# Letting GpSimd's weight differences wait for VectorE's sums of x, and moving one VectorE addition ahead of an h product

## The chip, the cores and the metric

The kernel runs on one core of one Trainium2 chip. The metric is device microseconds of one execution, the median over runs. A core has five engines with their own instruction queues: TensorE (PE, matmuls; PEld are its weight loads), VectorE (DVE), ScalarE (ACT), GpSimd (POOL) and SyncE (SP, which only issues DMAs here). Engines wait for each other through semaphores.

## What is computed

The reference is a retention recurrence (4 batches, 8 heads, 768 positions, head size 64) whose output, as 3072 tokens of width 512, goes through a bilinear feed-forward layer with hidden width 1536. The change lies wholly in the second half:

```python
def _attn_ref(q, k, v):
    ...
    for t in range(S):
        state = gamma * state + einsum('bhd,bhe->bhde', k[:, :, t], v[:, :, t])
        y[:, :, t] = scale * einsum('bhd,bhde->bhe', q[:, :, t], state)
    return y

def _moe_ref(x, w_a, w_b, w_out):
    a = x @ w_a
    b = x @ w_b
    return a * b @ w_out
```

## The kernel before

Tokens are taken in chunks of 128; 24 chunks form eight blocks J = 0..7 of 4, 2, 2, 2, 2, 4, 4, 4 chunks. For each block the recurrence (in a chunked form) leaves x transposed in the tile `xt[J]`. Then come 12 slices ft of the hidden width: `ffn_a` computes a = x·w_a into a PSUM bank and ScalarE copies it to `asb`; `ffn_g` computes g = x·w_b and VectorE multiplies the two into `ht` (line 629, called the h product below). The output stage `ffn_fast` multiplies `ht` with w_out for a pair of chunks at a time, u = 0, 1, by a scheme with seven products for eight; it needs four kinds of sums of `ht`, the tiles `hsum` (`add`, line 684, kinds 0 to 3), and adds the products up with VectorE and ScalarE through `snap` and `osb`.

Blocks 6 and 7 use the seven-product scheme for a = x·w_a too, for slices 2f and 2f+1 with f = 1..5. Its operands are

- the sums of x, `xs`: four VectorE additions and subtractions of `xt` (`combine_x`, line 695), for block 6 in the middle of the last output stage of block 5 (visit `(5, "sums", 1)`), for block 7 at its start;
- the differences of w_a, `ta`: four GpSimd subtractions for each f (`combine_a`, line 704), 20 in all, made once, from the visit `(5, "late", 0)` on.

`seven_a(J, f)` issues seven pairs of matmuls (`part_a`) into three banks R1, R2, R5, with two products g between them. `behind` holds what of one f is put behind the first matmuls of the next f: a VectorE addition (`plus(odd[:, W2:], R1, snap[:, 2])`, line 742) that reads the bank R1, and `last_of`, which adds part 4 into the same R1 and copies it out. Behind the last f there is no next one, so `seven_end` issues what is left, with the last two g between. `sums_of` gives the `hsum` of f − 1 to GpSimd; for block 6 all of them (f = 0 and 1 in one go of width 512), for block 7 those of f = 0 to 3 and kinds 0 and 1 of f = 4, VectorE doing the rest.

The order on each engine is the order of the code: `seq` ties every instruction to the one before it on its engine. The table `ahead` lists what is put in at named places (`visit`). `gate` makes the next GpSimd instruction wait for the VectorE instruction that was issued last; it stood in front of the vb casts of `(5, "late", 0)` before.

A PSUM bank is written anew only when its last reader is done. So in the output stage of block 5, u = 1, TensorE's last product, `product(R1, J, u, ("h", 1, 1), ...)`, waits for `plus(osb[:, 1, DH:], R1, snap[:, 3])`, which in VectorE's queue stands behind the four sums of x; and in `seven_end`, part 4 waits for the addition out of `behind`.

Of the kernel before, what the change touches and what calls it, by code (L numbers as in the profile page):

```python
# [12 lines left out]
ALU = mybir.AluOpType  # L13
# [14 lines left out]
def kernel(  # L28
# [10 lines left out]
    nc = tc.nc  # L39
# [38 lines left out]
    def seq(bi):  # L78
        ins = bi.ins
        if gates and ins.engine == mybir.EngineType.Pool:  # L80
            tc.add_manual_dep(ins, gates.pop(), after, reason="behind VectorE's sums")
        prev = last.get(ins.engine)
        if prev is not None:
            tc.add_manual_dep(ins, prev.name, nosync, reason="program order")
        last[ins.engine] = ins
        return bi
# [101 lines left out]
    def late_tables():  # L188
        seq(nc.gpsimd.memset(mask, 1.0))
        for c in range(2):  # L190
            mc = mask[64 * c : 64 * c + 64]
            seq(nc.gpsimd.affine_select(out=mc, in_=mc, compare_op=ALU.is_ge, fill=0.0, base=0,
                                        pattern=[[0, 1], [1, 2], [2, D // 2]],
                                        channel_multiplier=-1))
        return positions([[P, NCH], [0, 1]], 1), positions([[P, NCH], [0, 1]], 2, True)

    late = late_tables()
# [81 lines left out]
    def catch_up(n=100):  # L279
        for fn in later[:n]:  # L280
            fn()
        del later[:n]
# [5 lines left out]
    sums = {}  # L288
# [283 lines left out]
    def xcols(J, kt, c0, c1):  # L572
        W2 = 2 * P
        x = xt[J][:, c0 // W2 : (c1 + W2 - 1) // W2, kt].rearrange("p u par m -> p u (par m)")
        return x if c1 - c0 > W2 else x[:, 0, c0 % W2 : c0 % W2 + c1 - c0]
# [14 lines left out]
    ht = {}  # L590

    asbs = {}

    def parts(J, ft, c0, c1):

        if J == 0 and 2 <= ft < 10:
            return [(c0, (c0 + c1) // 2), ((c0 + c1) // 2, c1)]
        return [(c0, c1)]

    def ff_bank(J, ft, c, name):  # L600

        if (J, ft) in SPARE:
            return psat.tile([P, 4 * P], F32, tag=f"y{c}", name=name)
        return psff.tile([P, 4 * P], F32, tag="ff", name=name)

    def ffn_a(J, ft, c0=0, c1=None):
        c1 = TILES[J] * P if c1 is None else c1
        if J not in ht:
            ht[J] = htp.tile([P, NFT, 4 * P], BF16, tag="ht", name="ht")
        fs = slice(ft * P, (ft + 1) * P)  # L610
        a = ff_bank(J, ft, 0, "a")[:, : c1 - c0]
        for kt in range(KT):
            for b0, b1 in parts(J, ft, c0, c1):
                seq(nc.tensor.matmul(a[:, b0 - c0 : b1 - c0], wa_bf[:, kt, fs], xcols(J, kt, b0, b1),  # L614
                                     start=(kt == 0 and b0 == c0), stop=(kt == KT - 1 and b1 == c1),
                                     skip_group_check=True))
        asb = asbs[J, ft, c0] = asbp.tile([P, 4 * P], BF16, tag="asb", name="asb")[:, : c1 - c0]
        seq(nc.scalar.copy(asb, a))  # L618

    def ffn_g(J, ft, c0=0, c1=None):  # L620
        c1 = TILES[J] * P if c1 is None else c1
        fs = slice(ft * P, (ft + 1) * P)
        g = ff_bank(J, ft, 1, "g")[:, : c1 - c0]
        for kt in range(KT):
            for b0, b1 in parts(J, ft, c0, c1):
                seq(nc.tensor.matmul(g[:, b0 - c0 : b1 - c0], wb_bf[:, kt, fs], xcols(J, kt, b0, b1),  # L626
                                     start=(kt == 0 and b0 == c0), stop=(kt == KT - 1 and b1 == c1),
                                     skip_group_check=True))
        seq(nc.vector.tensor_tensor(ht[J][:, ft, c0:c1], g, asbs.pop((J, ft, c0)), op=ALU.mult))  # L629

    def ffn_ab(J, ft):
        ffn_a(J, ft)
# [6 lines left out]
    def store():  # L639
        for dst, src in held:  # L640
            seq(nc.sync.dma_start(out=dst, in_=src))
        held.clear()
# [45 lines left out]
    def combine_x(J):  # L688
        xs[J] = raw.tile([P, 4, 2, 2 * P], BF16, tag="q" * (J == 6) + "k" * (J == 7) + "f", name="xs")
        a11, a12, a21, a22 = (xt[J][:, u, 2 * c : 2 * c + 2].rearrange("p k par m -> p k (par m)")  # L690
                              for u in range(2) for c in range(2))
        s1, s2, s3, s4 = (xs[J][:, i] for i in range(4))
        for dst, x, y, op in ((s1, a21, a22, ALU.add), (s2, s1, a11, ALU.subtract),
                              (s4, a12, s2, ALU.subtract), (s3, a11, a21, ALU.subtract)):
            seq(nc.vector.tensor_tensor(dst, x, y, op=op))
# [12 lines left out]
    def own_banks(J):  # L708
        at = psat.tile([P, 2, 4 * P], F32, tag="at", name="a")
        st = psst.tile([P, 4 * P], F32, tag="st", name="a")  # L710
        y = [psat.tile([P, 4 * P], F32, tag=f"y{c}", name="a") for c in range(2)]
        banks[J] = [[y[f % 2][:, : 2 * P], st[:, : 2 * P], at[:, f % 2, : 2 * P]] for f in range(2)]

    def part_a(J, f, R, which, first):
        u, c, r, i = {1: (0, 0, 0, None), 2: (0, 1, 0, None), 3: (None, 1, 1, 3), 4: (1, 1, 3, None),
                      5: (None, None, 0, 0), 6: (None, None, 1, 1), 7: (None, None, 2, 2)}[which]
        for k in range(2):
            if which > 3:
                w = ta[r][:, k, f]
            else:  # L720
                w = wa_bf[:, 2 * c + k, (2 * f + r) * P : (2 * f + r + 1) * P]
            if i is None:
                x = xt[J][:, u, 2 * c + k].rearrange("p par m -> p (par m)")
            else:
                x = xs[J][:, i, k]
            seq(nc.tensor.matmul(R, w, x, start=(first and k == 0), stop=(k == 1),  # L726
                                 skip_group_check=True))

    def seven_a(J, f):

        W2 = 2 * P
        if J not in banks:
            own_banks(J)
        R1, R2, R5 = banks[J][f % 2]
        if (J, f) == (6, 1):
            R5 = psff.tile([P, 4 * P], F32, tag="ff", name="a")[:, :W2]
        snap = raw.tile([P, 4, W2], F32, tag="vf", name="snap")
        even, odd = (asbp.tile([P, 4 * P], BF16, tag="asb", name="asb") for _ in range(2))
        asbs[J, 2 * f, 0], asbs[J, 2 * f + 1, 0] = even, odd

        def plus(dst, R, x):
            seq(nc.vector.tensor_tensor(dst, R, x, op=ALU.add))  # L742

        part_a(J, f, R1, 1, True)
        seq(nc.scalar.copy(snap[:, 0], R1))  # L745
        part_a(J, f, R2, 2, True)
        part_a(J, f, R5, 5, True)
        seq(nc.scalar.copy(snap[:, 2], R5))
        for fn in behind[:1]:
            fn()  # L750
        plus(even[:, :W2], R2, snap[:, 0])
        catch_up(2)
        ffn_g(J, 2 * f - 1)
        part_a(J, f, R1, 6, False)
        seq(nc.scalar.copy(snap[:, 1], R1))
        for fn in behind[1:]:
            fn()
        behind.clear()
        part_a(J, f, R5, 3, False)
        plus(odd[:, :W2], R5, snap[:, 1])  # L760
        catch_up(2)
        ffn_g(J, 2 * f - 2)
        part_a(J, f, R1, 7, False)

        def last_of():
            part_a(J, f, R1, 4, False)
            seq(nc.scalar.copy(even[:, W2:], R1))

        behind.extend((lambda: plus(odd[:, W2:], R1, snap[:, 2]), last_of))

    behind = []

    def seven_end(J, f):
        behind[0]()
        ffn_g(J, 2 * f + 1)
        behind[1]()
        behind.clear()
        ffn_g(J, 2 * f)

    def product(R, J, u, left, right, first):  # L780
# [181 lines left out]
    for j in range(NO):  # L962
# [14 lines left out]
        (5, 0): [(casts, 20, "kq")], (5, 2): [(casts, 21, "kq"), (casts, 20, "v"), (casts, 21, "v")],  # L977
        (5, 3): [(turn, 16, None)], (5, 5): [(casts, 22, "kq")],
        (5, 6): [(casts, 23, "kq")], (5, 8): [(turn, 18, 16)],
        (5, "late", 0): [(gate,), (casts, 22, "v"), (casts, 23, "v")] + [(combine_a, f) for f in range(1, 6)],  # L980
        (5, "sums", 0): [(turn, 20, 18)], (5, "sums", 1): [(combine_x, 6)],
        (6, "a", 0): [(turn, 22, 20), (deal, 1, 0, 2, 3, 4), (catch_up, 2), (mask_now,)],
        (6, "o", 0): [(turn, None, 22)],
    }
# [18 lines left out]
    def blocks_seven(J):  # L1003
        f0, f1 = SEVEN[J]
        if J == 7:
            combine_x(J)
        store()
        for ft in range(2 * f0):
            ffn_a(J, ft)
            visit(J, "a", ft)  # L1010
        for f in range(f0, f1):
            seven_a(J, f)
            sums_of(J, f - 1)
            mask_now(1)
        seven_end(J, f1 - 1)
        sums_of(J, f1 - 1)
        return 2 * f1
# [77 lines left out]
```

## Time and profile before

| | |
|---|---|
| runs shown | 219.76, 219.34, 219.76 us; median 219.76 us |
| the profiled execution's own time | 219.66 us |
| its span, first to last instruction | 218.0 us, so 1.66 us lie around it |
| granted TensorE clock | 1.00 of full speed over the whole span |

Time by stage, busy microseconds of each engine:

| stretch, us | what runs | length | PE | DVE | ACT | POOL |
|---|---|---|---|---|---|---|
| 144.0 to 153.6 | output of block 5, sums of x, differences of w_a | 9.60 | 8.28 | 8.26 | 4.27 | 8.75 |
| 153.6 to 175.1 | block 6: a and g, recurrence of chunks 20 to 23 | 21.50 | 21.33 | 15.52 | 10.34 | 16.68 |
| 175.1 to 184.9 | output of block 6 | 9.80 | 9.80 | 4.49 | 3.53 | 3.81 |
| 184.9 to 205.0 | block 7: a and g | 20.10 | 20.00 | 15.24 | 7.99 | 11.69 |
| 205.0 to 218.0 | output of block 7, and the end | 13.00 | 9.47 | 4.58 | 2.98 | 0.00 |

A row of the timeline gives the start and the length of an instruction (or of several merged, with their count), engine, line, what is written and read, and in brackets the idle time ahead of it and what ended it. A row of the chain of waits gives start, length, engine, tile and line of one piece of the work that ended last. A matmul's length reaches past the start of the next one, since matmuls are pipelined.

### The profile page before, as it was taken

The page shows a single profiled execution, that of the slowest core. Times are in us where ns is not written, and L with a number is a line of the kernel's source. Part 1 is how long each engine was busy: PE and PEld are TensorE (multiplying, and loading weights), DVE is VectorE, ACT ScalarE, POOL GpSimd, SP SyncE. Part 2 cuts the span into 40 slices and gives each one's busy share as a digit, 9 for nine tenths or more (in the row PEclk, how much of TensorE's full clock was granted, in tenths as well). Part 3 has the DMA queues.
Part 4 walks back from the last instruction along what each step waited for, and adds up shares of the span by engine and source line. Part 5 has one row for each costly group of instructions (what it writes and reads, how often), then busy time and mean ns, then how long its engine had stood idle before and what let it go on. Part 6 is the DMA issues. An engine that isn't in the chain of part 4 may idle for free.

```text
span 218.0 us, 7107 instructions
## 1 busy us (share of the span) xinstructions
PE 209.2 (96%) x2886; PEld 157.0 (72%) x2889; DVE 147.5 (68%) x326; ACT 97.7 (45%) x247; POOL 129.5 (59%) x199
## 2 busy tenths in 40 slices
PE   6789999999999999999999999998999999999993
PEld 6578896785478888888887445486666588666682
DVE  2783547648938877786794587979577753777731
ACT  3675244342436446446475253735555242444231
POOL 6557789682737447572827573759929980087400
PEclk9999999999999999999999999999999999999999
DMA  5999999998998998899979899932200002200022
GB/s 171 347 376 383 370 310 381 357 206 174 238 234 195 292 256 179 200 266 189 188 164 273 187 276 215 203 75 98 101 0 0 3 0 99 98 2 3 0 96 96
DMA packets 94832, 39.77 MB, mean 182 GB/s; under 512 B 76112, under 2 KB 91728, under 8 KB 94800
## 3 DMA queue, kind: packets, MB, share of 16 engines
q1 hardware_dynamic: 94656, 39.20, 69.3%
q8 instruction: 22, 0.36, 0.7%
q10 hardware_dynamic: 144, 0.13, 0.2%
q14 instruction: 10, 0.08, 0.1%
HBM read 28.31 MB, written 6.29 MB: 159 GB/s over the span
## 4 chain that ended last, share of the span: by engine, by line
PE 90%; DMA 3%; DVE 2%; POOL 1%; ACT 1%; issue 1%; SPq 0%; POOLq 0%; DVEq 0%
PE g L626 28%; PE o L788 22%; PE a L614 21%; PE a L726 7%; PE o L661 5%; DMA kf<-in_k_dram 3%; PE y L375 2%; POOL kqb L245 1%; PE y L387 1%; PE at L330 1%; PE st L300 1%; DVE ht L629 1%; PE y L545 1%; PE tp L466 1%; PE st L507 1%
## 5 line engine op out<-in xcount | busy, mean ns | idle before, releaser
L629 DVE TENSOR_TENSOR ht<-g,asb 128x256 bf16<-128x256 f32 (+1 forms) x98 | 53.6, 548 | 36.4 <-PE g L626 29.9
L626 PE MATMUL g<-xt,wb_bf 128*128 128x256 bf16 (+1 forms) x424 | 77.7, 311 | 0.0
L614 PE MATMUL a<-xt,wa_bf 128*128 128x256 bf16 (+1 forms) x344 | 56.9, 295 | 0.1
L618 ACT CAST asb<-a 128x256 bf16<-128x256 f32 (+1 forms) x78 | 34.5, 443 | 47.6 <-PE a L614 46.3
L626 PEld LDWEIGHTS <-wb_bf 128*128 128x128 bf16 x424 | 41.3, 98 | 15.7
L614 PEld LDWEIGHTS <-wa_bf 128*128 128x128 bf16 x344 | 33.0, 98 | 10.9 <-DVE xt L209 0.4
L248 POOL TENSOR_TENSOR kqb<-kf,ktab 128x256 bf16<-128x256 f32 x28 | 17.5, 644 | 26.0 <-DMA kf<-in_k_dram 18.2
L788 PEld LDWEIGHTS <-hsum 128*128 128x128 bf16 x240 | 23.2, 98 | 2.9
L684 POOL TENSOR_TENSOR hsum<-ht 128x256 bf16<-128x256 bf16 (+1 forms) x19 | 13.7, 719 | 18.2 <-DVE ht L629 18.2
L800 ACT COPY snap<-o 128x256 f32<-128x256 f32 x38 | 14.2, 374 | 21.6 <-PE o L788 21.2
L209 POOL CAST vb<-vf 128x512 bf16<-128x512 f32 x30 | 17.9, 628 | 10.0 <-DMA vf<-in_v_dram 7.2
L788 PE MATMUL o<-wt_bf,hsum 128*128 128x256 bf16 x180 | 21.9, 273 | 0.0
L788 PEld LDWEIGHTS <-ht 128*128 128x128 bf16 x180 | 17.2, 98 | 4.6 <-issue 1.5
L248 POOL TENSOR_TENSOR kqb<-qf,qtab 128x256 bf16<-128x256 f32 x28 | 17.2, 635 | 3.6 <-DMA qf<-in_q_dram 3.5
L314 DVE TENSOR_TENSOR sums<-st,sums 128x256 f32<-128x256 f32 x30 | 12.7, 424 | 5.0 <-PE st L300 3.7
L788 PE MATMUL o<-wo_bf,ht 128*128 128x256 bf16 x120 | 14.9, 273 | 0.0
L207 ACT CAST gst<-sums 128x256 bf16<-128x256 f32 x33 | 12.8, 412 | 0.5 <-DVE sums L312 0.3
L803 DVE TENSOR_TENSOR osb<-o,snap 128x256 f32<-128x256 f32 x22 | 9.1, 416 | 5.6 <-ACT snap L800 3.7
L742 DVE TENSOR_TENSOR asb<-a,snap 128x256 bf16<-128x256 f32 x30 | 11.9, 418 | 1.1 <-ACT snap L745 0.9
L245 POOL TENSOR_TENSOR kqb<-kf,ktab 128x512 bf16<-128x512 f32 x7 | 7.7, 1107 | 8.0 <-DMA kf<-in_k_dram 7.7
L726 PEld LDWEIGHTS <-ta 128*128 128x128 bf16 x80 | 7.8, 98 | 6.1 <-issue 0.8
L336 DVE TENSOR_TENSOR aT<-at,mask 128x512 bf16<-128x512 f32 x18 | 12.1, 679 | 0.0
(100 smaller groups left out, 288.3 us busy)
## 6 DMA issues: line engine op xcount, KB each, us to landing
out_dram<-osb SPq DMA_DIRECT2D x11, 512.0 KB, 4.8
kf<-in_k_dram SPq DMA_DIRECT2D x18, 256.0 KB, 4.0
qf<-in_q_dram SPq DMA_DIRECT2D x36, 128.0 KB, 3.6
vf<-in_v_dram SPq DMA_DIRECT2D x18, 256.0 KB, 4.2
wsta<-in_moe_w_a_dram SPq DMA_DIRECT2D x6, 512.0 KB, 7.6
wstb<-in_moe_w_b_dram SPq DMA_DIRECT2D x6, 512.0 KB, 7.9
wsto<-in_moe_w_out_dram SPq DMA_DIRECT2D x6, 512.0 KB, 9.3
kf<-in_k_dram SPq DMA_DIRECT2D x3, 512.0 KB, 5.9
```

Source lines behind the costliest of these rows:

```text
L207: seq(nc.scalar.copy(dst, src))
L209: seq(engine.tensor_copy(dst, src))
L248: seq(eng.tensor_tensor(dst[:, r], src[:, r], tab[:, r], op=ALU.mult))
L314: seq(nc.vector.tensor_tensor(new, u[c][:, s], old, op=ALU.add))
L614: seq(nc.tensor.matmul(a[:, b0 - c0 : b1 - c0], wa_bf[:, kt, fs], xcols(J, kt, b0, b1), start=(kt == 0 and b0 == c0), stop=(kt == KT - 1 a ...
L618: seq(nc.scalar.copy(asb, a))
L626: seq(nc.tensor.matmul(g[:, b0 - c0 : b1 - c0], wb_bf[:, kt, fs], xcols(J, kt, b0, b1), start=(kt == 0 and b0 == c0), stop=(kt == KT - 1 a ...
L629: seq(nc.vector.tensor_tensor(ht[J][:, ft, c0:c1], g, asbs.pop((J, ft, c0)), op=ALU.mult))
L684: seq(eng.tensor_tensor(s[which], x(), y(), op=op))
L726: seq(nc.tensor.matmul(R, w, x, start=(first and k == 0), stop=(k == 1), skip_group_check=True))
L788: seq(nc.tensor.matmul(R[:, :DH], lhs, (wo_bf, wt_bf)[w][:, f, m, :], start=(first and f == 0), stop=(f == NH - 1), skip_group_check=True))
L800: seq(nc.scalar.copy(snap[:, i], R[:, :DH]))
```

## The change

Two edits.

1. In `ahead`, the sixteen GpSimd subtractions for f = 2 to 5 move from `(5, "late", 0)` to `(5, "sums", 1)`, behind `combine_x(6)` and a new `gate`. So GpSimd makes those of f = 1, and then waits for the fourth sum of x.
2. In the last `seven_a` of blocks 6 and 7 (`ends`), the addition from R1 is no longer left to `seven_end`: it is issued ahead of the h product of slice 2f − 2 = 8, which stood ahead of it.

```diff
-    def ffn_g(J, ft, c0=0, c1=None):
+    def ffn_g(J, ft, c0=0, c1=None, now=True):
...
-        seq(nc.vector.tensor_tensor(ht[J][:, ft, c0:c1], g, asbs.pop((J, ft, c0)), op=ALU.mult))
+        asb = asbs.pop((J, ft, c0))
+
+        def times():
+            seq(nc.vector.tensor_tensor(ht[J][:, ft, c0:c1], g, asb, op=ALU.mult))
+
+        if not now:
+            return times
+        times()
...
-    def seven_a(J, f):
+    def seven_a(J, f, ends=False):
...
-        ffn_g(J, 2 * f - 2)
+        times = ffn_g(J, 2 * f - 2, now=not ends)
         part_a(J, f, R1, 7, False)
...
         behind.extend((lambda: plus(odd[:, W2:], R1, snap[:, 2]), last_of))
+        if ends:
+            behind.pop(0)()
+            times()
...
     def seven_end(J, f):
-        behind[0]()
         ffn_g(J, 2 * f + 1)
-        behind[1]()
-        behind.clear()
+        behind.pop()()
         ffn_g(J, 2 * f)
...
-        (5, "late", 0): [(gate,), (casts, 22, "v"), (casts, 23, "v")] + [(combine_a, f) for f in range(1, 6)],
-        (5, "sums", 0): [(turn, 20, 18)], (5, "sums", 1): [(combine_x, 6)],
+        (5, "late", 0): [(gate,), (casts, 22, "v"), (casts, 23, "v"), (combine_a, 1)],
+        (5, "sums", 0): [(turn, 20, 18)], (5, "sums", 1): [(combine_x, 6), (gate,)] + [(combine_a, f) for f in range(2, 6)],
...
-            seven_a(J, f)
+            seven_a(J, f, f == f1 - 1)
```

GpSimd's queue around the differences of w_a, before: the four `ta` tiles (3374 to 3377) of f = 1, then those of f = 2; in brackets what a row waits for.

```order
L209 CAST vb_3106<-vf_2962 128x512 [waits DMAHW0_49,PE_49]
L704 TENSOR_TENSOR ta_3374<-wa_bf_172 128x2x128
L704 TENSOR_TENSOR ta_3375<-wa_bf_172,ta_3374 128x2x128 [waits Pool_49]
L704 TENSOR_TENSOR ta_3376<-wa_bf_172 128x2x128
L704 TENSOR_TENSOR ta_3377<-wa_bf_172,ta_3375 128x2x128 [waits Pool_49]
L704 TENSOR_TENSOR ta_3374<-wa_bf_172 128x2x128
L704 TENSOR_TENSOR ta_3375<-wa_bf_172,ta_3374 128x2x128 [waits Pool_49]
```

And of the change:

```order
L209 CAST vb_3106<-vf_2962 128x512 [waits DMAHW0_49,PE_49]
L711 TENSOR_TENSOR ta_3374<-wa_bf_172 128x2x128
L711 TENSOR_TENSOR ta_3375<-wa_bf_172,ta_3374 128x2x128 [waits Pool_49]
L711 TENSOR_TENSOR ta_3376<-wa_bf_172 128x2x128
L711 TENSOR_TENSOR ta_3377<-wa_bf_172,ta_3375 128x2x128 [waits Pool_49]
L711 TENSOR_TENSOR ta_3374<-wa_bf_172 128x2x128 [waits DVE_49]
L711 TENSOR_TENSOR ta_3375<-wa_bf_172,ta_3374 128x2x128 [waits Pool_49]
```

The queue holds the same instructions in the same order; the first one of f = 2 has gained a wait for VectorE, which is the fourth sum of x.

VectorE's queue at the end of block 7's stretch (`asb` 4390 is the odd half of f = 5, g 4416, 4427 and 4436 are those of slices 8, 11 and 10), before:

```order
L742 TENSOR_TENSOR asb_4390<-a_4224,snap_4388 128x256 [waits PE_49,Activation_49]
L629 TENSOR_TENSOR ht_4209<-g_4416,asb_4349 128x512 [waits PE_49,Activation_49]
L742 TENSOR_TENSOR asb_4390<-a_4227,snap_4388 128x256 [waits PE_49]
L629 TENSOR_TENSOR ht_4209<-g_4427,asb_4390 128x512 [waits DVE_49,PE_49]
L629 TENSOR_TENSOR ht_4209<-g_4436,asb_4389 128x512 [waits PE_49,Activation_49]
```

And of the change:

```order
L749 TENSOR_TENSOR asb_4390<-a_4224,snap_4388 128x256 [waits PE_49,Activation_49]
L749 TENSOR_TENSOR asb_4390<-a_4227,snap_4388 128x256 [waits PE_49]
L632 TENSOR_TENSOR ht_4209<-g_4416,asb_4349 128x512 [waits Activation_49]
L632 TENSOR_TENSOR ht_4209<-g_4427,asb_4390 128x512 [waits DVE_49,PE_49]
L632 TENSOR_TENSOR ht_4209<-g_4436,asb_4389 128x512 [waits PE_49,Activation_49]
```

The h product of slice 8 and the addition from R1 have changed places; block 6 has the same exchange. TensorE's queue is the same in both kernels, but for a wait for VectorE at the first output product into the bank that held the g of slice 8.

## The prediction

> **What bounds the kernel now.** I read the page first, for the engine that sets the end, then the chain of waits for the places where that engine stands still, then the timeline around them.
>
> ```profile
> span 218.0 us, 7107 instructions
> PE 209.2 (96%) x2886; PEld 157.0 (72%) x2889; DVE 147.5 (68%) x326; ACT 97.7 (45%) x247; POOL 129.5 (59%) x199
> PE 90%; DMA 3%; DVE 2%; POOL 1%; ACT 1%; issue 1%; SPq 0%; POOLq 0%; DVEq 0%
> ```
>
> TensorE is busy for 96% of the span and makes up 90% of the chain, so only what closes a gap of TensorE shortens the time. Behind 148 us the chain leaves TensorE for VectorE at three places that matter here:
>
> ```profile
> 151.60 0.88 DVE xs L695
> 152.87 0.81 PE o L788 x6
> ...
> 173.56 0.34 DVE asb L742
> 173.94 0.38 PE a L726 x2
> ...
> 202.77 0.69 DVE ht L629
> 203.84 0.38 PE a L726 x2
> ```
>
> The first is the last product of block 5, which waits for a sum of x and the osb addition behind it. The other two are part 4 at the ends of blocks 6 and 7, which wait for the asb addition, which itself stands behind the h product of slice 8. Each edit aims at one kind of place.
>
> **Edit 1, the sums of x.** The timeline of VectorE, GpSimd and TensorE there:
>
> ```profile
> 149.54 0.52 DVE L695 TENSOR_TENSOR xs<-xt 128x512 bf16<-128x512 bf16 x1
> 149.74 0.85 POOL L704 TENSOR_TENSOR ta<-wa_bf 128x256 bf16<-128x256 bf16 x1
> 150.10 0.77 DVE L695 TENSOR_TENSOR xs<-xs,xt 128x512 bf16<-128x512 bf16 x1
> 150.73 0.82 PE L788 MATMUL o<-wo_bf,hsum 128*128 128x256 bf16 x6
> 150.91 0.78 DVE L695 TENSOR_TENSOR xs<-xt,xs 128x512 bf16<-128x512 bf16 x1
> 151.60 0.88 DVE L695 TENSOR_TENSOR xs<-xt 128x512 bf16<-128x512 bf16 x1
> 152.41 0.74 DVE L803 TENSOR_TENSOR osb<-o,snap 128x256 f32<-128x256 f32 x2
> 152.87 0.81 PE L788 MATMUL o<-wt_bf,ht 128*128 128x256 bf16 x6 [1.32 <-DVE osb L803]
> ```
>
> The same four operations for block 7, with GpSimd idle:
>
> ```profile
> 185.49 0.41 DVE L695 TENSOR_TENSOR xs<-xt 128x512 bf16<-128x512 bf16 x1
> 185.94 0.43 DVE L695 TENSOR_TENSOR xs<-xs,xt 128x512 bf16<-128x512 bf16 x1
> 186.40 0.42 DVE L695 TENSOR_TENSOR xs<-xt,xs 128x512 bf16<-128x512 bf16 x1
> 186.74 0.42 DVE L695 TENSOR_TENSOR xs<-xt 128x512 bf16<-128x512 bf16 x1
> ```
>
> Beside GpSimd's differences three of the sums take 0.77 to 0.88 us, alone 0.41 to 0.43: the two engines slow each other where both read two operands from SBUF. The difference of the two rows is a contention that the gate removes, since GpSimd's differences of f = 2 start only behind the fourth sum, and those of f = 1 are done by then (the row at 149.74 is the third of f = 2).
>
> The page "SBUF — State Buffer" of the Trainium skill, section "SBUF: two separate sides", calls the port that the two share an exclusive lock: the loser is blocked for the other's whole instruction. By that rule each of these sums would wait for a whole difference of 0.67 us and be about 1.09 us apart (an estimate from that page's rule). The rows above show steps of 0.56 to 0.81 us, less than that, so the trace bears the contention out but not a full block each time; the sum uses the measured lengths, and would be the same by the rule, which leaves the sums alone once the gate stands.
>
> With block 7's steps the fourth sum starts 1.25 us (185.49 to 186.74) behind the first, at 150.79, and the osb addition 0.34 (186.40 to 186.74) later, at 151.13. It takes 0.41 (half of "0.74 x2", with 0.33 between starts), and TensorE starts 0.05 behind its end, as 152.41 + 0.41 = 152.82 did to 152.87: 151.59 instead of 152.87, **1.28 us** earlier. Bounds: TensorE itself is free at 150.73 + 6 × 0.109 = 151.38 (the step is that of the weight loads quoted below), so at most 1.49; if the first sum keeps its 0.52 for another reason than GpSimd, 1.18. I take 1.28, since the shape is the same.
>
> What the move costs on GpSimd:
>
> ```profile
> 152.98 0.66 POOL L704 TENSOR_TENSOR ta<-wa_bf 128x256 bf16<-128x256 bf16 x1
> 158.85 0.67 POOL L704 TENSOR_TENSOR ta<-wa_bf,ta 128x256 bf16<-128x256 bf16 x1
> 160.23 0.38 PE L726 MATMUL a<-xs,ta 128*128 128x256 bf16 x2
> 169.99 0.38 PE L726 MATMUL a<-xs,ta 128*128 128x256 bf16 x2
> 163.87 1.16 POOL L684 TENSOR_TENSOR hsum<-ht 128x512 bf16<-128x512 bf16 x1 [4.35 <-DVE ht L629]
> ```
>
> The ten differences from 152.98 to 158.85 start 0.652 us apart. The sixteen now start at about 151.21 + 0.08 = 151.29 (the end of the fourth sum, and the 0.08 that GpSimd needs to follow VectorE, shown below) and end at 151.29 + 15 × 0.652 + 0.67 = 161.74. First, TensorE took the first weights of f = 2 at 160.23 and those of f = 5 at 169.99, and would want them 1.28 earlier, at 158.95 and 168.71; they are there by 153.9 and 161.7, so no weight is late. Second, queued behind them on GpSimd is the first hsum of block 6, which starts when its h products are there: 163.87 − 1.28 = 162.59. GpSimd is free 0.85 us earlier. The 4.35 us of idle time before that row are what hides the move. No DMA and no other instruction is moved; SP's queue is the same.
>
> **Edit 2, the end of the stretch in block 6.** All times here are those of before; the shift of 1.28 changes none of the distances.
>
> ```profile
> 171.73 1.03 PE L626 MATMUL g<-xt,wb_bf 128*128 128x512 bf16 x4
> 172.59 0.38 PE L726 MATMUL a<-xs,ta 128*128 128x256 bf16 x2
> 172.81 1.03 PE L626 MATMUL g<-xt,wb_bf 128*128 128x512 bf16 x4
> 172.86 0.69 DVE L629 TENSOR_TENSOR ht<-g,asb 128x512 bf16<-128x512 f32 x1 [0.44 <-PE g L626]
> 173.47 0.41 DVE L742 TENSOR_TENSOR asb<-a,snap 128x256 bf16<-128x256 f32 x1
> 173.69 0.67 POOL L684 TENSOR_TENSOR hsum<-ht 128x256 bf16<-128x256 bf16 x1
> 173.99 0.69 DVE L629 TENSOR_TENSOR ht<-g,asb 128x512 bf16<-128x512 f32 x1
> ...
> 177.06 0.67 POOL L684 TENSOR_TENSOR hsum<-hsum,ht 128x256 bf16<-128x256 bf16 x1
> 177.62 2.61 PEld L788 LDWEIGHTS <-hsum 128*128 128x128 bf16 x24
> 177.73 2.13 PE L788 MATMUL o<-wt_bf,hsum 128*128 128x256 bf16 x18
> ```
>
> VectorE follows TensorE by 0.10 (171.73 + 1.03 = 172.76 to 172.86). Part 7 ends at 172.59 + 0.38 = 172.97, so the addition, now first, runs from 173.07 to 173.49, and part 4 could start 0.06 later (173.47 + 0.41 to 173.94), at 173.55. TensorE is free from its g at 172.81 + 0.86 (the step from 171.73 to 172.59) = 173.67. So the gap from 173.67 to 173.94 goes: **0.27 us**.
>
> What is late next is the h product of slice 8: it starts 0.33 behind the addition, at 173.40, and ends at 174.09 instead of 173.55. The product of slice 11 behind it moves by only 0.02 (173.40 + 0.61 = 174.01). But GpSimd's hsum of f = 4 reads slice 8; it started at 173.69, close behind the 173.55. It follows VectorE by 0.08:
>
> ```profile
> 202.72 1.03 PE L626 MATMUL g<-xt,wb_bf 128*128 128x512 bf16 x4
> 203.54 0.67 POOL L684 TENSOR_TENSOR hsum<-ht 128x256 bf16<-128x256 bf16 x1 [0.59 <-DVE ht L629]
> ```
>
> (202.77 + 0.69 = 203.46 to 203.54). So it starts at 174.17, 0.48 later, and with it the gapless queue behind it, in which the sum of kind 1 for f = 5, at 177.06 before, is the sixth. That now ends at 177.06 + 0.48 + 0.67 = 178.21, and TensorE can have it at 178.29, taking the same 0.08. TensorE loads it as the sixth of the hsum weights: at 177.62 + 5 × 0.109 (2.61 / 24) = 178.16 before, and 0.27 earlier now, 177.89. It would wait 0.40. The gain of 0.27 turns into a loss: **0.27 − 0.40 = −0.13 us**. The last sums, 0.63 and 1.26 later on GpSimd, are wanted 1.3 and 2.0 later, so they add nothing. Bounds: +0.27 if that wait is not there, −0.21 if GpSimd's end counts another 0.08 late. I take −0.13, from the rows.
>
> The page "Perfetto Trace Analysis" of the Trainium skill, section "GPSIMD Engine Instruction", warns that a GpSimd span is unreliable, and to go by the spacing of starts. By spacing (0.63 here, an estimate) instead of the span of 0.67 the wait would be 0.36 and the whole 0.04 us better; the rows of GpSimd here overlap by just that 0.04, which bears the warning out, and it decides nothing.
>
> **Edit 2 in block 7.** The same exchange: TensorE is free at 202.72 + 0.86 = 203.58 and started part 4 at 203.84, **0.26 us**. GpSimd's hsum of f = 4 starts 0.5 later there too, but idle time of 0.59 lay ahead of it, it has only two operations there, and the sums wanted last are VectorE's, behind the h product of slice 10, which comes 0.26 earlier with its g. So I count the 0.26 in full; bounds 0 and 0.26.
>
> **Sum.** 1.28 − 0.13 + 0.26 = 1.41 us. The profiled execution took 219.66 us in all, 1.66 around its span of 218.0; so 218.25. Its own time is 0.10 under the median of the runs shown, so I forecast 218.3 for the median. Bounds: 1.49 + 0.27 + 0.26 = 2.02 gives 217.6, 1.18 − 0.21 + 0 = 0.97 gives 218.7.
>
> **The rivals.** *The hidden wait is not there* (20%): GpSimd's late start in block 6 is made good, or the weights are taken a little later, and all three gaps close: 1.81 us, 217.9. For it: 0.40 is a difference of small numbers. Against it: GpSimd's queue has no idle time from 163.87 to its end, so nothing can be made good.
>
> *The gate does nothing* (9%): the sums of x are slow for another reason, xt just written or TensorE's traffic. Then 0 − 0.13 + 0.26 = 0.13 us, 219.6. Against it stand the lengths of GpSimd itself, 0.85 beside the sums and 0.66 behind them.
>
> *GpSimd becomes the bound* (5%), the case on the other side: the differences, pushed together behind the gate, run slowly beside VectorE's additions and the hsum queue starts late. If they end at T, that queue's sum of kind 1 for f = 5 ends at T + (177.06 + 0.67 − 163.87) = T + 13.86, and TensorE wants it at 177.89 − 1.28 = 176.61, less 0.08. The wait, T − 162.67, eats the 1.81 us from T = 164.48 on, which is a step of 0.83 us instead of 0.652. The contended steps were 0.81. At 0.90 T is 165.46, the wait 2.79, the loss 0.98: 220.7. Against it: 0.652 was measured beside the same VectorE additions and h products that it meets now.
>
> **How the numbers follow.** Forecast 66%, rivals 20%, 9%, 5%. The range is 217.5 to 218.9: both bounds, the first rival's 217.9, and the spread of 0.4 us of the runs shown above the slower bound; left out are the other two rivals and a little at both ends. A measurement of this kernel can tell about 0.2% from no change, 0.44 us. The forecast and the first rival are faster by more, 86%; the second is within, 9%; the third slower, 5%.
>
> **What would show it.** The four sums of x near 150 us at 0.41 to 0.43 and TensorE's idle time in front of the last product of block 5 near 0.1 instead of 1.32 show edit 1 right; sums that are still 0.77 show it wrong. Part 4 without idle time in front at the ends of both stretches shows edit 2 right. A new idle stretch of about 0.4 us within the hsum products of block 6, released by GpSimd, shows the price; its absence gives the first rival. GpSimd still at its differences when the h product of slice 3 of block 6 is done would make the forecast wrong towards slow, and so would an osb addition that waits for something other than the sums of x.

## The result, and the profile after

| | before | changed |
|---|---|---|
| median of the runs | 219.96 us (219.34 to 220.79) | 218.59 us (218.36 to 218.91) |
| the profiled execution | 219.66 us | 218.87 us |
| its span | 218.0 us | 217.2 us |

The ratio is 0.9936, 95% interval 0.9913 to 0.996: the change is faster by 1.4 us (0.9 to 1.9). The forecast was 218.3, the range 217.5 to 218.9. Ratios and intervals, here and below, leave out two disturbed executions (222.61 and 307.86 us) and are not the quotients of the medians.

The page of the changed kernel, first its span and then the shares of the chain of waits by engine:

```profile
span 217.2 us, 7105 instructions
...
PE 89%; DMA 3%; DVE 3%; POOL 1%; ACT 1%; issue 1%; SPq 0%; DVEq 0%; POOLq 0%
```

TensorE still sets the time. The two profiled executions differ by only 0.79 us, less than the medians, and the reason lies ahead of the change. The first row of the chain of waits in which data moves, in the changed kernel:

```profile
1.93 6.29 DMA kf<-in_k_dram
```

and in the kernel before:

```profile
1.93 5.95 DMA kf<-in_k_dram
```

The first load took 0.34 us longer in this execution, and some more such differences follow; by 150 us it stands 0.79 us behind the other (the row of TensorE at 151.52 below against 150.73 before), in code that is the same. So I compare lengths from that row on. It is the fourth hsum product of block 5 (the six matmuls that read wo_bf and hsum), which TensorE issues just ahead of the first gap. The timeline there, changed kernel:

```profile
150.33 0.41 DVE L702 TENSOR_TENSOR xs<-xt 128x512 bf16<-128x512 bf16 x1
150.78 0.42 DVE L702 TENSOR_TENSOR xs<-xs,xt 128x512 bf16<-128x512 bf16 x1
151.24 0.42 DVE L702 TENSOR_TENSOR xs<-xt,xs 128x512 bf16<-128x512 bf16 x1
151.52 0.82 PE L796 MATMUL o<-wo_bf,hsum 128*128 128x256 bf16 x6
151.58 0.42 DVE L702 TENSOR_TENSOR xs<-xt 128x512 bf16<-128x512 bf16 x1
151.91 0.89 DVE L811 TENSOR_TENSOR osb<-o,snap 128x256 f32<-128x256 f32 x2
152.07 0.67 POOL L711 TENSOR_TENSOR ta<-wa_bf 128x256 bf16<-128x256 bf16 x1 [2.87 <-DVE xs L702]
152.38 0.82 PE L796 MATMUL o<-wt_bf,ht 128*128 128x256 bf16 x6
```

The four sums of x take 0.41 to 0.42 us, GpSimd stands still for 2.87 us behind its first four differences and goes on 0.07 behind the fourth sum, and the last product starts 0.86 behind the fourth hsum product instead of 2.14 (150.73 to 152.87): 1.28 us won.

The end of the stretch of block 6 and its output, changed kernel (the rows of PEld are the weight loads):

```profile
172.10 0.38 PE L733 MATMUL a<-xs,ta 128*128 128x256 bf16 x2
172.32 1.03 PE L626 MATMUL g<-xt,wb_bf 128*128 128x512 bf16 x4
172.52 0.42 DVE L749 TENSOR_TENSOR asb<-a,snap 128x256 bf16<-128x256 f32 x1 [0.59 <-PE a L733]
172.87 1.28 DVE L632 TENSOR_TENSOR ht<-g,asb 128x512 bf16<-128x512 f32 x2
173.19 0.38 PE L733 MATMUL a<-xt,ta 128*128 128x256 bf16 x2
173.63 0.67 POOL L691 TENSOR_TENSOR hsum<-ht 128x256 bf16<-128x256 bf16 x1 [0.38 <-DVE ht L632]
...
176.87 0.53 PEld L796 LDWEIGHTS <-hsum 128*128 128x128 bf16 x5
176.98 2.35 PE L796 MATMUL o<-wt_bf,hsum 128*128 128x256 bf16 x18
177.01 0.67 POOL L691 TENSOR_TENSOR hsum<-hsum,ht 128x256 bf16<-128x256 bf16 x1
177.73 1.97 PEld L796 LDWEIGHTS <-hsum 128*128 128x128 bf16 x19 [0.32 <-POOL hsum L691]
```

Part 4 (173.19) follows the g without a gap, 0.87 behind its start; it was 1.13 before (172.81 to 173.94): 0.26 won. The new wait is there too: GpSimd starts its hsum of f = 4 late behind the h product of slice 8, and the sixth weight load waits 0.32 us for it. The eighteen products take 2.35 instead of 2.13: 0.22 lost.

The end of block 7 in the changed kernel, and the last product:

```profile
202.18 1.03 PE L626 MATMUL g<-xt,wb_bf 128*128 128x512 bf16 x4
203.05 0.38 PE L733 MATMUL a<-xt,ta 128*128 128x256 bf16 x2
...
212.86 0.81 PE L796 MATMUL o<-wt_bf,ht 128*128 128x256 bf16 x6
```

No gap either: 0.87 instead of 1.12 (202.72 to 203.84), 0.25 won. The last product of the kernel before:

```profile
213.65 0.81 PE L788 MATMUL o<-wt_bf,ht 128*128 128x256 bf16 x6
```

From the fourth hsum product of block 5 to the last product it is 62.92 us before (150.73 to 213.65) and 61.34 now (151.52 to 212.86), 1.58 less. This **stretch** leaves out what differs ahead of it; I give it for every run.

### The profile page after: what moved, and what is told of

Same layout as the page of the kernel before. It is cut to its first block, busy times and chain, and to the rows that moved or that the text cites. A ratio compares the mean times of both kernels' runs of the same rounds, so it can differ in the third digit from the quotient of the medians.

```text
span 217.2 us, 7105 instructions
## 1 busy us (share of the span) xinstructions
PE 209.5 (96%) x2886; PEld 156.9 (72%) x2889; DVE 148.0 (68%) x326; ACT 97.7 (45%) x247; POOL 130.0 (60%) x199
## 4 chain that ended last, share of the span: by engine, by line
PE 89%; DMA 3%; DVE 3%; POOL 1%; ACT 1%; issue 1%; SPq 0%; DVEq 0%; POOLq 0%
PE g L626 29%; PE a L614 20%; PE o L796 20%; PE a L733 7%; PE o L668 5%; DMA kf<-in_k_dram 3%; PE y L375 2%; PE y L387 1%; POOL kqb L245 1%; PE st L300 1%; PE at L330 1%; PE y L545 1%; PE tp L466 1%; DVE ht L632 1%; DVE xs L702 1%
```

## The experiments

The question was which part makes the gain, whether the sums are slow through GpSimd, and what holds the sixth hsum weight. The kernel before, run beside them, had a median of 219.91 us beside the first four experiments and of 219.93 beside the last four.

| kernel | median, us | ratio to before, interval | stretch, us | less than before |
|---|---|---|---|---|
| before (profile above) | 219.96 | | 62.92 | |
| the change | 218.59 | 0.9936, 0.9913 to 0.996 | 61.34 | 1.58 |
| the gate alone | 218.88 | 0.9947, 0.9919 to 0.9975 | 61.70 | 1.22 |
| without the gate | 219.89 | 1.0009, 0.9987 to 1.0031 | 62.51 | 0.41 |
| all differences behind the gate | 219.85 | 1.0003, 0.9979 to 1.0026 | 62.74 | 0.18 |
| new order of eight GpSimd sums | 218.24 | 0.9921, 0.9891 to 0.9951 | 61.12 | 1.80 |
| sums of x earlier, no gate | 218.27 | 0.9929, 0.9911 to 0.9947 | 61.59 | 1.33 |
| gate, order and earlier sums | 217.88 | 0.9919, 0.9895 to 0.9943 | 61.00 | 1.92 |
| copies in place of differences | 218.97, one execution | | 62.00 | 0.92 |
| long differences | 226.77, one execution | | 69.94 | 7.02 more |

**The gate alone.** Only the table `ahead`, on the kernel before:

```diff
-        (5, "late", 0): [(gate,), (casts, 22, "v"), (casts, 23, "v")] + [(combine_a, f) for f in range(1, 6)],
-        (5, "sums", 0): [(turn, 20, 18)], (5, "sums", 1): [(combine_x, 6)],
+        (5, "late", 0): [(gate,), (casts, 22, "v"), (casts, 23, "v"), (combine_a, 1)],
+        (5, "sums", 0): [(turn, 20, 18)], (5, "sums", 1): [(combine_x, 6), (gate,)] + [(combine_a, f) for f in range(2, 6)],
```

> Edit 1 alone, on the kernel before. If GpSimd's differences beside the sums of x cost the 1.28 us, the four sums take 0.41 to 0.43 us each, TensorE stands still for about 0.2 us instead of 1.5 us in front of the last product of block 5, the gaps of 0.27 and 0.26 us at the ends of the two stretches stay, there is no idle time at the hsum weights of block 6, and the time is 1.3 us shorter than before (ratio 0.994). If the gain of the whole change comes from edit 2, this kernel gains nothing.

Faster, ratio 0.9947, and the stretch 1.22 us shorter. The gap at the end of block 6 is as before, and the hsum weights come in one run of 24 without a wait; TensorE and its loads in this kernel:

```profile
173.20 1.03 PE L626 MATMUL g<-xt,wb_bf 128*128 128x512 bf16 x4
174.33 0.38 PE L726 MATMUL a<-xt,ta 128*128 128x256 bf16 x2
178.01 2.61 PEld L788 LDWEIGHTS <-hsum 128*128 128x128 bf16 x24
```

So the gate makes the greater part of the gain, and the wait for the hsum weight belongs to edit 2. That edit 2 adds anything, the clock does not show (0.9947 and 0.9936 lie within each other's intervals); the stretch does, with 0.36 us.

**Without the gate.** The change, with

```diff
-        ... (5, "sums", 1): [(combine_x, 6), (gate,)] + [(combine_a, f) for f in range(2, 6)],
+        ... (5, "sums", 1): [(combine_x, 6)] + [(combine_a, f) for f in range(2, 6)],
```

> The change without its gate: the sixteen differences are written behind the sums in the code, but nothing holds GpSimd back, so its queue is that of before; edit 2 stays. If contention is what the gate removes, the sums are again at 0.77 to 0.88 us, TensorE's idle time in front of the last product of block 5 is back at 1.3 us, and what is left is edit 2: about 0.05 us at the end of block 6 (0.27 won, 0.2 lost in a wait for the hsum weights) and 0.26 us at the end of block 7, so 0.3 us in all (ratio 0.9986, hardly to be told from 1). If the place in the code alone made the gain, it is as fast as the change.

No faster than before by the clock (1.0009), 0.41 us in the stretch. The sums are slow again, and TensorE waits again:

```profile
150.02 0.77 DVE L702 TENSOR_TENSOR xs<-xs,xt 128x512 bf16<-128x512 bf16 x1
150.83 0.78 DVE L702 TENSOR_TENSOR xs<-xt,xs 128x512 bf16<-128x512 bf16 x1
151.53 0.88 DVE L702 TENSOR_TENSOR xs<-xt 128x512 bf16<-128x512 bf16 x1
152.80 0.81 PE L796 MATMUL o<-wt_bf,ht 128*128 128x256 bf16 x6 [1.21 <-DVE osb L811]
```

The place in the code does nothing by itself; the semaphore does. Of the 0.41, 0.11 lie ahead of this last product: the first sum and a difference started in the same moment (149.57), and here the sum went first, with 0.41 us, and the difference took 0.94. The other 0.30 are edit 2: 0.26 at the end of each of blocks 6 and 7, less 0.22 at the hsum weights, where this kernel waits too.

**All differences behind the gate.** The change, with `combine_a` of f = 1 moved behind the gate as well:

```diff
-        (5, "late", 0): [(gate,), (casts, 22, "v"), (casts, 23, "v"), (combine_a, 1)],
+        (5, "late", 0): [(gate,), (casts, 22, "v"), (casts, 23, "v")],
-        ... [(combine_x, 6), (gate,)] + [(combine_a, f) for f in range(2, 6)],
+        ... [(combine_x, 6), (gate,)] + [(combine_a, f) for f in range(1, 6)],
```

> The change with the four differences of f = 1 behind the gate too. The sums of x and the gaps stay as in the change. If GpSimd has only 0.76 us to spare in front of the hsum of block 6, as the idle time there in the change says, four more operations of 0.65 us make its first hsum 1.9 us late, 0.4 us of which the idle time in front of the hsum of f = 4 takes up, and TensorE waits about 1.7 us (0.2 + 1.5) for the sixth hsum weight: 1.5 us slower than the change, about as slow as the kernel before (ratio 1.000). If the queue has more room than that, it is as fast as the change.

As slow as before (1.0003). Four operations more are what GpSimd's slack cannot hide:

```profile
176.44 0.71 PE L796 MATMUL o<-wt_bf,hsum 128*128 128x256 bf16 x5
178.59 1.59 PE L796 MATMUL o<-wt_bf,hsum 128*128 128x256 bf16 x13 [1.45 <-POOL hsum L691]
```

After five products TensorE stops until 178.59; the sixth was due at 176.44 + 5 × 0.109 = 176.99, so it lost 1.6 us, 1.4 more than in the change. This is the rival of a GpSimd that becomes the bound, and it shows how near the change stands to it.

**A new order of eight GpSimd sums.** The change, with kinds 0 and 1 of f = 4 and 5 of block 6 ahead of kinds 2 and 3:

```diff
+            if f == 4:
+                return
             f0, f1 = (0, 2) if f == 1 else (f, f + 1)
+            if f == 5:
+                for pair in ((0, 1), (2, 3)):
+                    for g in (4, 5):
+                        for which in pair:
+                            add(J, which, g, g + 1, nc.gpsimd)
+                return
```

> The change with another order of GpSimd's last eight sums of block 6: kinds 0 and 1 of f = 4 and f = 5 first, then kinds 2 and 3. If the wait of 0.2 us at the hsum weights of block 6 is only due to the late start behind the h product of slice 8, the kind 1 sum of f = 5 ends some 1.2 us earlier, that wait is gone, and no other takes its place (kind 3 of f = 5 ends at the same time as before): the output of block 6 is 0.2 us shorter, ratio to before 0.9925 against the 0.9936 of the change. If something else holds those weights, the wait stays.

The wait is gone, TensorE's eighteen products and the weight loads run through, and the stretch is 0.22 us shorter than with the change:

```profile
176.26 2.61 PEld L796 LDWEIGHTS <-hsum 128*128 128x128 bf16 x24
176.37 2.13 PE L796 MATMUL o<-wt_bf,hsum 128*128 128x256 bf16 x18
```

By the clock the difference to the change (0.9921 against 0.9936) lies within the intervals; only the trace shows it.

**The sums of x earlier, without the gate.** Is it the gate that counts, or the place of the osb addition in VectorE's queue? The four sums go ahead of the first osb addition, and two mask products (`mask_now`, the rows `aT<-at,mask`) that stood ahead of the sums go behind the last one.

```diff
+        visit(J, "x", u)
         plus(osb[:, 0, :DH], R2, snap[:, 0])
...
-        mask_now(1)
+        if J != 5:
+            mask_now(1)
...
-        mask_now()
+        if (J, u) != (5, 0):
+            mask_now()
...
-        ... (5, "sums", 1): [(combine_x, 6), (gate,)] + [(combine_a, f) for f in range(2, 6)],
+        ... (5, "x", 1): [(combine_x, 6)] + [(combine_a, f) for f in range(2, 6)],
```

> The change without its gate, but with the four sums of x written earlier on VectorE: ahead of the first osb addition of the last output stage of block 5, and the two mask products of chunk 20 behind the last osb addition of that stage. If what costs is only that the osb addition stands behind slow sums in VectorE's queue, the sums may stay slow (0.77 to 0.88 us beside GpSimd, starting some 1.2 us earlier, at 148.1 in the clock of before) and TensorE's idle time in front of the last product still falls from 1.5 to about 0.5 us: about 1.0 + 0.3 = 1.3 us faster than before (ratio 0.994), nearly what the gate gives. If the gate is needed, this kernel is as slow as the one without the gate (ratio 1.000).

Faster, 0.9929, with slow sums:

```profile
149.46 0.78 DVE L702 TENSOR_TENSOR xs<-xt,xs 128x512 bf16<-128x512 bf16 x1
150.16 0.89 DVE L702 TENSOR_TENSOR xs<-xt 128x512 bf16<-128x512 bf16 x1
150.65 0.82 PE L796 MATMUL o<-wo_bf,hsum 128*128 128x256 bf16 x6
151.77 0.82 PE L796 MATMUL o<-wt_bf,ht 128*128 128x256 bf16 x6 [0.30 <-DVE osb L811]
```

The contention is as great as ever, but the last sum ends 0.40 us behind the start of the hsum product (150.65 to 151.05) instead of 1.75 (150.73 to 152.48), so 1.12 lie between the two products instead of 2.14: 1.02 won. It is the two mask products that make the room, since all four sums stand ahead of the awaited osb addition in both kernels. In the kernel before they stood ahead of it:

```profile
147.68 0.68 DVE L336 TENSOR_TENSOR aT<-at,mask 128x512 bf16<-128x512 f32 x1
148.61 0.68 DVE L336 TENSOR_TENSOR aT<-at,mask 128x512 bf16<-128x512 f32 x1
149.21 0.41 DVE L803 TENSOR_TENSOR osb<-o,snap 128x256 f32<-128x256 f32 x1
```

Each held VectorE for 0.60 us (148.61 to 149.21), 1.20 together. Some of that was lost again, because the first sum now takes 0.67 instead of 0.52. So the slow sums cost time only because TensorE waited for what was queued behind them. A kernel with the mask products moved and the sums left in their place was not run.

**Gate, order and earlier sums together.** The edits of the last two, with the gate kept behind `combine_x`.

> All together: the gate, the order of GpSimd's last eight sums with kinds 0 and 1 first, and the earlier sums of x with the mask products behind. The sums take 0.42 us each from about 148.1 (clock of before), so the osb addition waits only for TensorE and the last product of block 5 starts 0.07 us behind the one before instead of 0.21 in the change; no idle time at the hsum weights of block 6. From the start of the last three-fold product of block 5 to the end 0.14 us less than with the new order of the sums alone, 0.36 less than with the change: 1.9 us less than before (ratio 0.991). If the mask products behind hold up the scores of chunks 22 and 23, TensorE gains an idle time in front of them instead.

The lowest median, 217.88 us, ratio 0.9919 (0.9895 to 0.9943), which the clock cannot tell from the change or the two kernels above. The stretch is the shortest, 61.00, 1.92 less than before and 0.34 less than with the change:

```profile
150.84 0.82 PE L796 MATMUL o<-wo_bf,hsum 128*128 128x256 bf16 x6
151.59 0.81 PE L796 MATMUL o<-wt_bf,ht 128*128 128x256 bf16 x6
```

0.75 between the two products, against 0.65 for six matmuls back to back; no new idle time in front of the scores.

**Copies in place of differences.** To see what GpSimd has to do to slow VectorE, in the kernel before; the differences are left out, so only the times count:

```diff
-            seq(nc.gpsimd.tensor_tensor(dst, x, y, op=ALU.subtract))
+            seq(nc.gpsimd.tensor_copy(dst, x))
```

> The kernel before, with GpSimd copying one operand where it subtracted two (the differences of w_a are left out, so a of blocks 6 and 7 is another; the time is that of the rest). If any GpSimd operation that reads SBUF slows VectorE's sums with their two operands, the sums that meet copies are still longer than 0.5 us. If it takes two operands on both sides, all four are at 0.42 us and TensorE's idle time in front of the last product of block 5 is about 0.2 us.

```profile
146.43 7.67 POOL L704 COPY ta<-wa_bf 128x256 bf16<-128x256 bf16 x20
149.77 0.42 DVE L695 TENSOR_TENSOR xs<-xt 128x512 bf16<-128x512 bf16 x1
150.22 0.50 DVE L695 TENSOR_TENSOR xs<-xs,xt 128x512 bf16<-128x512 bf16 x1
150.76 0.50 DVE L695 TENSOR_TENSOR xs<-xt,xs 128x512 bf16<-128x512 bf16 x1
151.18 0.61 DVE L695 TENSOR_TENSOR xs<-xt 128x512 bf16<-128x512 bf16 x1
```

The copies, 0.40 us each by the median of the twenty, also lengthen the sums, though less: 0.50, 0.50 and 0.61. So the first reading holds: on GpSimd's side one operand is enough. The two of 0.50 lie on the line that I had set, the last clearly above it. The last two products of block 5 are 1.22 us apart (150.96 to 152.18), against 0.86 in the change and 2.14 before. One execution, no verdict on the time.

**Long differences.** In the kernel before, the sixteen differences as four, each over f = 2 to 5:

```diff
+            b11, b12, b21, b22 = (w[:, c, r, 2:6] for c in range(2) for r in range(2))
+            t1, t2, t3, t4 = (t[:, :, 2:6].rearrange("p k f m -> p f k m") for t in ta)
```

> The kernel before, with the sixteen differences of f = 2 to 5 as four operations of four times the width, about 2.1 us each (from 0.67 for width 256 and 1.15 for 512). If the port between the two engines is locked for a whole instruction, each of the four sums of x waits for a whole difference: they start some 2.5 us apart and end near 158 us in the clock of before, and TensorE stands still for 5 us or more. If the engines share it in small pieces, the sums stay at 0.77 to 0.88 us, the idle time at 1.5 us, and the time is that of before.

One execution: 226.77 us, 6.8 above the median of before. TensorE waited 6.8 us in front of the last product of block 5. That the two figures agree is chance: before, TensorE waited there too, and the products are 7.59 us apart (150.81 to 158.40) instead of 2.14, 5.45 more. The rest comes behind the wait: the granted TensorE clock is 0.50 of full speed from 158.4 to 162.2 us, and the six products and what follows, up to the a of the next slice, take 4.58 us (158.40 to 162.98) instead of 3.01 (152.87 to 155.88), 1.57 more; with the 5.45 that is the 7.02 of the stretch. VectorE and GpSimd:

```profile
149.61 1.64 DVE L695 TENSOR_TENSOR xs<-xt 128x512 bf16<-128x512 bf16 x1
151.05 2.18 POOL L708 TENSOR_TENSOR ta<-wa_bf,ta 128x1024 bf16<-128x1024 bf16 x1
151.28 2.22 DVE L695 TENSOR_TENSOR xs<-xs,xt 128x512 bf16<-128x512 bf16 x1
153.19 2.29 POOL L708 TENSOR_TENSOR ta<-wa_bf 128x1024 bf16<-128x1024 bf16 x1
153.54 2.22 DVE L695 TENSOR_TENSOR xs<-xt,xs 128x512 bf16<-128x512 bf16 x1
```

The sums are as long as the differences beside them, each ends 0.27 to 0.28 us behind one (151.05 + 2.18 = 153.23, and 151.28 + 2.22 = 153.50), and they start 1.7 to 2.3 us apart. That is a lock for a whole instruction.

## Why the prediction was right, point by point

**What bounds the kernel.** Right: the three gaps of TensorE named there are the three that closed, the first but for 0.21 us. With the new wait they make up the whole stretch: 1.28 + 0.26 − 0.21 + 0.25 = 1.58.

**Edit 1, 1.28 us.** Right in the mechanism, and to the hundredth in this profile (0.86 between the two products instead of 2.14); the hundredth is partly luck, since the gate alone gave 1.22 in its stretch, with 0.93 between the products. The contention was the cause: without the gate the sums are slow again and the gain is gone. The slack of GpSimd was predicted at 0.85 us; the profile of the changed kernel has 0.76 of idle time ahead of the first hsum, and the run with all differences behind the gate bears that out: four more, 4 × 0.66 us, less the 0.76 and the 0.38 of idle time ahead of the hsum of f = 4, leave 1.5, and TensorE lost 1.4.

**Edit 2 in block 6, −0.13 us.** The mechanism was right, the size of one term was not. "It would wait 0.40" was 0.21 us of TensorE, so the term came to 0.26 − 0.21 = +0.05. Two things in it were off. I counted the wait from the moment at which the weight load was wanted; but a load runs 0.11 us ahead of its product (176.87 and 176.98), so a load that is 0.32 late delays the product by only 0.21 (due at 176.98 + 5 × 0.109 = 177.52, started at 177.73). The other 0.08 are the delays that I had set: GpSimd's hsum of f = 4 came 0.43 late instead of 0.48 in that clock, and TensorE followed GpSimd's end (177.01 + 0.67 = 177.68) by 0.05, not 0.08. That the wait is the price of the late h product of slice 8 is shown by the new order of the sums: it takes the wait away and gains the 0.22.

**Edit 2 in block 7, 0.26 us.** Right: 0.87 between g and part 4 instead of 1.12, 0.25 us, and TensorE waits nowhere behind it.

**The sum.** 1.41 was forecast; the ratio gives 1.4, the stretch 1.58. The 0.17 between forecast and stretch is the mis-sized wait, +0.05 instead of −0.13, less the 0.01 of block 7. That the clock gives the forecast's own 1.4 is luck: its interval is 0.9 to 1.9, and holds 1.58 as well. The median itself, 218.59, lies 0.29 above the forecast, 0.20 of it because the kernel before came out at 219.96 in these runs and not at the 219.76 from which I counted.

**The rivals.** That the hidden wait is not there fell: it is there, at half the size. That the gate does nothing fell with the run without it. GpSimd as the bound fell for the change, but four operations more bring it about. The break-even was a step of 0.83 us for its operations, and the differences ran at 0.66 (152.07 to 161.96 in fifteen steps) where 0.652 was forecast.

**The aside on the lock.** Its estimate of 1.09 us for sums that wait for whole differences, and the reading that the trace shows "not a full block each time", were wrong; they did not enter the sum. The long differences show the full block that the page "SBUF — State Buffer" of the Trainium skill, section "SBUF: two separate sides", states. My estimate had added the whole 0.42 of a sum to the 0.67 of a difference, but a sum is done 0.28 us after the difference that holds it up, and GpSimd loses only about 0.16 per pair (steps of 0.81 instead of 0.652). The rows quoted in the prediction say the same: the difference at 149.74 ends at 150.59, the sum at 150.10 ends at 150.87. The prediction also had both engines slow each other "where both read two operands from SBUF"; the copies show that GpSimd needs only one.

## What to carry to other kernels

Look at the whole queue ahead of the awaited instruction before making one slow instruction fast: here keeping GpSimd away from VectorE's sums won 1.28 us, and taking two mask products out from ahead of the awaited addition won 1.02 us with the sums left slow. When an instruction is put ahead of another on one engine, follow the one that falls back to every engine that reads it; the h product that gave way cost 0.43 us of GpSimd's start and 0.2 us of TensorE in the output stage that follows, and reordering GpSimd's queue by the order in which TensorE wants its results won that back. Where two engines lock each other out for whole instructions, short instructions on the engine that can wait keep the price small.

## What the runs showed of the hardware

VectorE's sums, with two SBUF operands, and GpSimd's differences and copies exclude each other for the whole instruction. Beside differences of width 1024 (2.13 us, the first row of them in the trace of the long differences) a sum of 0.42 us takes 2.2 to 2.3, beside differences of width 256 (0.67) 0.77 to 0.88, beside copies (0.40) 0.5 to 0.6; it ends some 0.28 us behind the GpSimd instruction. Where a sum went first (without the gate, at 149.57), it took 0.41 and the difference 0.94. VectorE's additions that read one operand from PSUM kept their 0.41 to 0.42 us beside the same differences.

In the trace of the long differences TensorE stood still from 151.6 to 158.4 us. Its granted clock was 1.00 up to 155 us, 0.50 from 156 to 162.2, and 1.00 again from 162.4 on. Behind the 1.32 us of idle time in the kernel before it stayed at 1.00.
